# Four attention layers on one core: the second layer's first query chunk cut into four key parts

## The chip, the cores and the metric

One core of a Trainium2 chip runs the whole program. The metric is device time in microseconds (us) of one execution, and the figure of a kernel is the median of several executions.

## The reference

Four residual attention layers follow each other on x of 2048 x 640, with 32 heads of width 20. Layers 0 and 2 use the weights A and a sliding window of 256 keys; layers 1 and 3 use the weights B and attend to all 2048 keys.

```python
x = x + A(layernorm(x)); x = x + B(layernorm(x))
x = x + A(layernorm(x)); x = x + B(layernorm(x))
# A, B: qkv = x @ wqkv; p = softmax(mask(q k^T * 20**-0.5)); out = (p v) @ wo
# mask in A alone: 0 <= i - j < 256
```

## The kernel before

**Work is cut into units.** A unit (layer l, query chunk c, head group g) covers 512 queries (c = 0..3) and four heads (g = 0..7). Its scores are counted in banks: one bank is one head, 128 keys by 512 queries, one PSUM bank of f32. A unit of a windowed layer has 12 banks, a unit of a full layer 64 (16 key blocks of 128, times four heads). The first query chunk of layers 1 and 3 is cut in two parts by `SPLIT`: in layer 1 part "a" has key blocks 0 to 7 and part "b" blocks 8 to 15, 32 banks each.

**The order is one list, `units`, written out by hand.** Before the change: layer 0's chunks 0 to 2; then layer 0's chunk 3, with part "a" of one group of layer 1 after each of its groups 1, 2, 3, 4 and 6; then the three left-over "a" parts; then the eight "b" parts; then layers 1, 2 and 3. A part of layer 1 can start only when its keys exist, and keys of chunk c exist only when layer 0 is finished for that chunk.

**Tiles.** The banks of the list, in order, are cut into tiles of three; while `narrow` holds (layer 0 and part "a"), tiles of three and two alternate. For each tile the scores are made by TensorE (PE, L848), the exp by ScalarE (ACT, L862) straight from PSUM into `pt`, the window mask is multiplied in by VectorE (DVE, L887) in the windowed layers, and two or three tiles later the products with the values are added up in `op`, one single PSUM bank (PE, L905). At the end of a unit `finish_unit` copies `op` away on DVE: part "a" into the f32 tile `raw_o` (L709), part "b" adds it to `raw_o` (L721), other units at L723. The tail then normalises (`t_tail`, L745 to L773).

**Other work hangs between the tiles.** Projections of queries and keys (L323, evacuated by `evac`, L267 on ACT or L269 on DVE), of values (L410), layer norm (L342 to L374) and output projection (L491, L500) are tasks in a list sorted by `need`, the index of the unit that needs them first. After each tile `pump` gives them a credit of `rate(t)`: 1.2 while layer 0 works on chunks 0 to 2, else what it takes to finish the tasks 16 tiles ahead of their need, times 1.1, from 0.66 to 0.9 in the early stage. The credit is in an estimate of full-clock PE microseconds that is written into the tasks. If a unit starts while something that it needs is not made, `require` emits all of that at once, with no tile between. Two PSUM banks, 5 and 6, serve these tasks while tiles are narrow; later only bank 6.

**Layer 1's operands go through DRAM.** `t_full` and `t_v` write queries, keys and values out (L470, L431); `load_unit` brings a part's keys, queries and values back: one DMA for values (L644), four for queries (L655) and four for keys (L657). All these are issued by SyncE's queue (SP), in program order. `load_ahead` looks once per tile at the next unit of a full layer and loads it, if what it needs was made and a buffer is free (three for keys and for values, four for queries).

**Evacuation.** `state["act"]` decides who evacuates projections: ACT while layer 0 is in chunks 0 to 2, DVE from then on.

Of the kernel before, what the change touches and what calls it, by code (L numbers as in the profile page):

```python
# [11 lines left out]
ALU = mybir.AluOpType  # L12
# [7 lines left out]
NT = S // P  # L20
KD = D // P
G = 8
C = 512
NC = S // C
# [1 line left out]
SCALE = DH ** -0.5  # L26
HD = D // 2
VW = DH + 1
SPLIT = {1: 8, 3: 12}


@with_exitstack
def kernel(
# [10 lines left out]
    nc = tc.nc  # L44
# [44 lines left out]
    op = ps[:, 7, :]  # L89
# [16 lines left out]
    def load_wop(w):  # L106
# [7 lines left out]
        out=ident[:], in_=ident[:], compare_op=ALU.not_equal, fill=1.0,  # L114
# [38 lines left out]
    state = {"tick": 0, "held": None, "credit": 0.0, "early": True, "act": True, "unit": 0}  # L153
# [16 lines left out]
    def push(name, gen, need, left):  # L170
        insort(todo, Task(name, gen, need, left))

    def push_tail(name, gen):
        tails.append(Task(name, gen, 0, 0.0))
# [286 lines left out]
    def t_full(l, n, c, b):  # L461

        while ("xnT", l, c) not in ready:
            yield ("wait", 1)
        yield from room("w")
        wt = yield from take_w(l, n, c, b)
        yield from project(wt, xnT[l, c], staged)
        rows = slice(b * P, (b + 1) * P)
        dst = k_d[l][rows, c * C : (c + 1) * C] if n else q_d[l][c, rows, :]
        nc.sync.dma_start(out=dst, in_=staging.pop())  # L470
        live["w"] -= 1
        used(l, c)
        ready.add(("qk"[n], l, c, b))
# [63 lines left out]
    def push_layer(l, c):  # L537

        need = [first_use(l, c, g) for g in range(G)]
        push(("ln", l, c), t_ln(l, c), need[0], 1.6)  # L540
        if l % 2:
            halves = ((0,), (1,)) if l == 1 else ((0, 1),)
            for h in halves:
                push(("v", l, c, *h), t_v(l, c, h), need[4 * h[0]], 2.8 * len(h))
            for b in range(KD):
                g = b * P // 80
                for n in (1, 0):
                    worder[l, n].append((l, n, c, b))
                    first = need[g] if n else index[l, c, g, "a" if c == 0 else None]
                    push(("qk"[n], l, c, b), t_full(l, n, c, b), first, 1.1)  # L550
            return
        for g in range(G):
            for n in (0, 1):
                worder[l, n].append((l, n, c, g))
            push(("qk", l, c, g), t_qk_window(l, c, g), need[g], 2.2)
            if g == 0:
                push(("v", l, c), t_v(l, c, (0, 1)), need[0], 5.6)


    def key_blocks(l, part):  # L560
        return {None: (0, NT), "a": (0, SPLIT.get(l)), "b": (SPLIT.get(l), NT)}[part]

    class Unit:
        def __init__(self, l, c, g, part=None):
# [43 lines left out]
            (1, 2, [(2, 2, 2, 2)]),  # L608
        ]

    units = [Unit(0, c, g) for c in range(NC - 1) for g in range(G)]
    early = deque(Unit(1, 0, g, "a") for g in range(G))
    for g in range(G):
        units.append(Unit(0, NC - 1, g))
        if g in (1, 2, 3, 4, 6):
            units.append(early.popleft())
    units += early
    units += [Unit(1, 0, g, "b") for g in range(G)]
    for c in range(1, NC + 1):
        small = deque(Unit(2, c - 1, g) for g in range(G))  # L620
        for g in range(G):
            units.append(Unit(1, c, g) if c < NC else Unit(3, 0, g, "a"))
            for _ in range(((0, 0, 2, 2, 2, 2, 0, 0) if c < NC else (0, 0, 2, 3, 3, 0, 0, 0))[g]):
                units.append(small.popleft())
    units += [Unit(3, 0, g, "b") for g in range(G)]
    units += [Unit(3, c, g) for c in range(1, NC) for g in range(G)]
    full = [u for u in units if not u.windowed]
    place = {id(u): n for n, u in enumerate(full)}
    index = {(u.l, u.c, u.g, u.part): n for n, u in enumerate(units)}

    def first_use(l, c, g):

        if l % 2 == 0:
            return index[l, c, g, None]
        return index[l, 0, g, "a" if 4 * c < SPLIT[l] else "b"]

    def load_unit(u):

# [62 lines left out]
    part_o = {}  # L701

    def finish_unit(u):
        l, c, g = u.l, u.c, u.g
        if u.part == "a":
            if not part_o:
                part_o["t"] = big.tile([P, G, C], F32, name="raw_o", tag="early_late")
            raw_o = part_o["t"]
            nc.vector.tensor_copy(out=raw_o[:, g, :], in_=op)  # L709
            return  # L710
        if (l, c) not in ons:
            for ll, cc in list(ons):
                if len(ons) >= 2:
                    require(("out", ll, cc))
            ons[l, c] = onp.tile([P, G, C], BF16, name="on", tag="on")
        on = ons[l, c]
        while len(tails) >= 3:
            require(("tail", *tails[0].name[1:]))
        oT = otp.tile([P, C], BF16, name="oT", tag="oT")
        if u.part == "b":  # L720
            nc.vector.tensor_tensor(out=oT[:], in0=part_o["t"][:, g, :], in1=op, op=ALU.add)  # L721
        else:
            nc.vector.tensor_copy(out=oT[:], in_=op)  # L723
        push_tail(("tail", l, c, g), t_tail(l, c, g, on, oT))
# [59 lines left out]
    def t_stats0(c):  # L784
        for i in range(4):
            stats(0, c, i)
            yield ("pe", 0.1)
        ready.add(("x", 0, c))

    with tc.manual_schedule():  # L790
# [3 lines left out]
        require(("qk", 0, 0, 0))  # L794

        def narrow(u):
            return u.l == 0 or (u.l, u.part) == (1, "a")

        banks = [b for u in units for b in u.banks]
        tiles = []  # L800
# [1 line left out]
        n = 0  # L802
# [7 lines left out]
        def rate(t):  # L810

            u = tiles[t][0][0]
            if u.l == 0 and u.c < NC - 1:
                return 1.2
            done, r = 0.0, 0.6 if state["early"] else 0.35
            for task in todo:
                done += max(task.left, 0.0)
                if task.need < len(units):
                    r = max(r, done / max(starts[id(units[task.need])] - t - 16, 1))
            return min(1.1 * r, 0.9)  # L820

        started = set()
        pts = deque()
# [1 line left out]
        for t in range(len(tiles) + 8):  # L825
            state["tick"] += 1
            n_b = 0
            if t < len(tiles):
                cur = tiles[t]
                n_b = len(cur)  # L830
                for b in cur:
                    u = b[0]
                    if id(u) not in started:
                        started.add(id(u))
                        if u.l == 0 and u.g == 0 and u.c + 1 < NC and u.c not in pushed:
                            pushed.add(u.c)
                            push(("stats", u.c + 1), t_stats0(u.c + 1), index[0, u.c + 1, 0, None], 0.4)
                            push_layer(0, u.c + 1)
                        state["unit"] = index[u.l, u.c, u.g, u.part]
                        state["act"] = u.l == 0 and u.c < NC - 1  # L840
                        if state["early"] and not narrow(u):
                            end_early()
                        start_unit(u)
                sp = ps[:, 0:3, :] if t % 2 == 0 else ps[:, 3:6, :]
                for n in range(2):
                    for i, (u, j, m, b0, subs, first, last, end) in enumerate(cur):
                        for kc, q0, qn, col in subs[n : n + 1]:
                            nc.tensor.matmul(  # L848
                                sp[:, i, col * P : (col + qn) * P],
                                lhsT=u.k(kc, j), rhs=u.q(j, q0, qn), start=True, stop=True,  # L850
                            )
                for b in cur:
                    if b[-1]:
                        s_emitted(b[0])
                pt = ptp.tile([P, 3, C], BF16, name="pt", tag="pt")
                i = 0
                while i < n_b:
                    b0 = cur[i][3]
                    k = i
                    while k < n_b and cur[k][3] == b0:  # L860
                        k += 1
                    nc.scalar.activation(  # L862
                        out=pt[:, i:k, b0 * P :], in_=sp[:, i:k, b0 * P :],
                        func=ACT.Exp, scale=SCALE,
                    )
                    i = k
                for i, b in enumerate(cur):
                    pts.append((t, pt, i, b))
                load_ahead()
                r = rate(t)  # L870
                pump(r, r + 0.1)
            else:
                pump(2.0, 2.0)

            if 0 < t <= len(tiles):
                cur_, pt_ = masked
                i = 0
                while i < len(cur_):
# [4 lines left out]
                    if m is not None:  # L883
# [4 lines left out]
                            out=pt_[:, i:k, b0 * P :], in0=pt_[:, i:k, b0 * P :], in1=mv_,  # L888
                            op=ALU.mult,
# [5 lines left out]
            if len(pts) >= 4 and pts[3][0] <= t - (3 if pts[0][3][0].windowed else 2):  # L895
                group = [pts.popleft() for _ in range(4)]
                u, subs, end = group[0][3][0], group[0][3][4], group[3][3][7]
                first, last = group[0][3][5:7]
# [50 lines left out]
```

The softmax here doesn't subtract the row's maximum and nothing guards it: scores larger than these inputs give would overflow.

## Time and profile before

| | |
|---|---|
| median of 4 runs | 2542.0 us (2521.11 to 2548.67) |
| the profiled execution | 2535.62 us |
| its span, first to last instruction | 2533.9 us |
| PE / ACT / DVE busy | 2096.8 / 2259.5 / 831.1 us |
| exp instructions on ACT (L862) | 1695, 2201.2 us |
| moved over the DMA queues | 118.78 MB |

The profile's rows name engines (PE is TensorE, PEld its weight loads, DVE VectorE, ACT ScalarE, POOL GpSimd, SP SyncE) and lines (L862 is line 862 of the kernel). PEclk is the granted TensorE clock, 1.00 or 10 tenths being full speed. A row by stretches gives start and end in us, the length, then the busy time and the number of instructions of each engine, the clock and the DMA share. The matmuls' ends are modelled, so that a busy PE isn't PE at its peak.

Unit ends are seen as DVE's copies of `op`. By these, layer 0's chunk 0 is finished at 102.3 us, its unit (chunk 1, group 4) at 151.0, the second unit of its chunk 3 at 286.9, its last unit at 414.6; the eight "a" parts at 474.8, the first "b" part at 493.7 and all eight at 594.8.

### The profile page before, as it was taken

The numbers are of one execution on the slowest core, as the hardware profiler recorded it, in microseconds if no ns is written. First come the engines' busy times: TensorE is split into PE (matmuls) and PEld (weight loads), VectorE is DVE, ScalarE is ACT, GpSimd is POOL, SyncE is SP. The second block draws the span as 40 slices with busy tenths as digits, with TensorE's granted clock in tenths as the row PEclk, the third lists the DMA queues.
The fourth block names the chain that finished last, engine by engine and source line by source line (L and its number), as shares of the span: only waits on it lengthen the run. The fifth ranks groups of instructions, "written<-read, shape, count | busy, mean of one in ns | idle before, by whom it ended". The sixth has DMA issues, their size and how long they took to land.

```text
span 2533.9 us, 37494 instructions
## 1 busy us (share of the span) xinstructions
PE 2096.8 (83%) x15184; PEld 727.4 (29%) x15184; DVE 831.1 (33%) x1895; ACT 2259.5 (89%) x1819; POOL 39.4 (2%) x112
## 2 busy tenths in 40 slices
PE   7888998888888888788888888888877787777777
PEld 3344333222222333223322233232222222222222
DVE  5676664212333334243334333442210011001001
ACT  5777788799889898999888988898999999999997
POOL 1000000000000000000000000000000000000000
PEclk9899997756755689658885579668565555557556
DMA  4111431311200113002221032103210011001000
GB/s 146 55 33 43 115 82 42 86 39 44 61 23 25 36 43 98 23 25 51 57 69 35 1 86 73 33 11 82 59 32 25 25 37 34 24 25 35 24 25 11
DMA packets 134974, 118.78 MB, mean 47 GB/s; under 512 B 64528, under 2 KB 122256, under 8 KB 134800
## 3 DMA queue, kind: packets, MB, share of 16 engines
q1 hardware_dynamic: 134800, 116.38, 17.1%
q8 instruction: 119, 1.95, 0.3%
q14 instruction: 55, 0.45, 0.1%
HBM read 95.09 MB, written 21.23 MB: 46 GB/s over the span
## 4 chain that ended last, share of the span: by engine, by line
ACT 44%; PE 28%; issue 12%; DVE 6%; DMA 0%; SPq 0%; ACTq 0%; POOL 0%; DVEq 0%
ACT pt L862 43%; PE ps L323 8%; PE ps L848 7%; PE ps L905 5%; PE ps L491 4%; PE ps L410 3%; DVE pt L887 2%; PE ps L374 1%; DVE st L269 1%; PE ps L769 1%; DVE qa L269 0%; DVE oT L723 0%; PE ps L522 0%; DVE ka L269 0%; DVE x_sb L500 0%
## 5 line engine op out<-in xcount | busy, mean ns | idle before, releaser
L862 ACT ACTIVATE pt<-ps 128x1536 bf16<-128x1536 f32 (+2 forms) x1695 | 2201.2, 1531 | 215.7 <-PE ps L848 192.8
L848 PE MATMUL ps<-qt,kt 20*128 20x512 bf16 x4096 | 739.6, 521 | 300.4 <-ACT pt L862 288.4
L905 PE MATMUL ps<-pt,vt 128*21 128x512 bf16 x4096 | 551.2, 524 | 9.2 <-DVE oT L723 5.2
L848 PEld LDWEIGHTS <-kt 20*128 20x128 bf16 x4096 | 206.4, 96 | 784.1 <-issue 769.2
L323 PE MATMUL ps<-xnT,wqk 128*128 128x512 bf16 x1040 | 318.0, 448 | 17.2 <-DMA wqk<-in_B_wqkv_dram 3.4
L887 DVE TENSOR_TENSOR pt<-pt,masks 128x1024 bf16<-128x1024 bf16 (+5 forms) x404 | 240.2, 624 | 218.2 <-ACT pt L862 217.8
L723 DVE CAST oT<-ps 128x512 bf16<-128x512 f32 x112 | 76.8, 685 | 443.8 <-PE ps L905 443.3
L905 PEld LDWEIGHTS <-vt 128*21 128x21 bf16 x4096 | 107.9, 92 | 347.9 <-issue 344.9
L491 PE MATMUL ps<-wop,on 128*128 128x320 bf16 x968 | 179.0, 336 | 3.8 <-DVE x_sb L500 1.9
L848 PE MATMUL ps<-qa,ka 32*128 32x384 bf16 (+2 forms) x1408 | 139.9, 328 | 37.4 <-ACT pt L862 31.9
L323 PEld LDWEIGHTS <-wqk 128*128 128x128 bf16 x1040 | 100.1, 108 | 170.8 <-issue 106.4
L500 DVE TENSOR_TENSOR x_sb<-x_sb,ps 128x320 bf16<-128x320 bf16 x120 | 58.2, 486 | 227.9 <-PE ps L491 227.5
L410 PE MATMUL ps<-wv,xnT 128*128 128x320 bf16 x640 | 120.2, 328 | 9.2 <-ACT xnT L267 2.1
L773 DVE TENSOR_TENSOR on<-oT,ps 128x512 bf16<-128x512 bf16 x128 | 87.7, 685 | 95.7 <-PE ps L769 94.1
L491 PEld LDWEIGHTS <-on 128*128 128x128 bf16 x968 | 94.7, 107 | 74.8 <-issue 32.2
L905 PE MATMUL ps<-pt,va 128*21 128x384 bf16 (+2 forms) x1408 | 92.5, 333 | 14.4 <-DVE oT L723 12.7
L269 DVE CAST st<-ps 128x512 bf16<-128x512 f32 x76 | 52.5, 690 | 127.7 <-PE ps L323 125.6
L750 DVE RECIPROCAL rz<-ps 128x16 f32<-128x16 f32 x128 | 32.8, 256 | 179.1 <-PE ps L745 168.8
L848 PEld LDWEIGHTS <-ka 32*128 32x128 bf16 x1408 | 41.3, 97 | 122.7 <-issue 112.3
L410 PEld LDWEIGHTS <-xnT 128*128 128x128 bf16 x640 | 59.9, 104 | 55.6 <-issue 31.9
L769 PE MATMUL ps<-rT,spread 32*128 32x128 bf16 x512 | 67.5, 270 | 4.4 <-DVE rT L762 3.9
L769 PEld LDWEIGHTS <-spread 32*128 32x128 bf16 x512 | 48.9, 118 | 27.9 <-issue 24.1
(54 smaller groups left out, 649.7 us busy)
## 6 DMA issues: line engine op xcount, KB each, us to landing
wqk<-wqk_d SPq DMA_DIRECT2D x112, 160.0 KB
vt<-v_d SPq DMA_DIRECT2D x48, 336.0 KB
kt<-k_d SPq DMA_DIRECT2D x192, 80.0 KB
wqk<-in_B_wqkv_dram SPq DMA_DIRECT2D x80, 160.0 KB
qt<-q_d SPq DMA_DIRECT2D x320, 20.0 KB
v_d<-vs SPq DMA_DIRECT2D x16, 336.0 KB
k_d<-st SPq DMA_DIRECT2D x40, 128.0 KB
q_d<-st SPq DMA_DIRECT2D x40, 128.0 KB
```

The source lines that it names most:

```text
L269: nc.vector.tensor_copy(out=out_, in_=in_)
L323: nc.tensor.matmul(pq, lhsT=wt[:, dc, :], rhs=xt[:, dc, :], start=(dc == 0), stop=(dc == KD - 1),)
L410: nc.tensor.matmul(pv, lhsT=xt[:, dc, i * P : (i + 1) * P], rhs=wv_sb[l % 2][:, dc, h * HD : (h + 1) * HD], start=(dc == 0), stop=(dc == K ...
L491: nc.tensor.matmul(yp, lhsT=on[:, g, qb * P : (qb + 1) * P], rhs=wop[:, g, i * HD : (i + 1) * HD], start=(last or g == 0), stop=(g == G - 1),)
L500: nc.vector.tensor_tensor(out=xv, in0=had, in1=yp, op=ALU.add)
L723: nc.vector.tensor_copy(out=oT[:], in_=op)
L769: nc.tensor.matmul(zb[:, qb * P : (qb + 1) * P], lhsT=spread4[:, qb, :], rhs=rT[:], start=True, stop=True,)
L773: nc.vector.tensor_tensor(out=on[:, g, :], in0=oT[:], in1=zb, op=ALU.mult)
L848: nc.tensor.matmul(sp[:, i, col * P : (col + qn) * P], lhsT=u.k(kc, j), rhs=u.q(j, q0, qn), start=True, stop=True,)
L862: nc.scalar.activation(out=pt[:, i:k, b0 * P :], in_=sp[:, i:k, b0 * P :], func=ACT.Exp, scale=SCALE,)
L887: nc.vector.tensor_tensor(out=pt_[:, i:k, b0 * P :], in0=pt_[:, i:k, b0 * P :], in1=mv_, op=ALU.mult,)
L905: nc.tensor.matmul(op[32 * j : 32 * j + VW, q0 * P : (q0 + qn) * P], lhsT=u.v(kc, j), rhs=pt[:, i, col * P : (col + qn) * P], start=(first ...
```

## The change

The two-way split of layer 1's first chunk becomes four parts of four key blocks, each as long as one query chunk of layer 0. Parts 0, 1 and 2 of all eight groups (24 units of 16 banks) are put one by one behind layer 0's units, from chunk 1, group 5 on; 19 find a place there and the other five follow, then the eight parts 3. Layer 3's split stays as it was. A part takes its keys from one chunk alone, so that part 0 can start when layer 0's chunk 0 is through.

With it come: `raw_o` is added to by the middle parts; tiles stay narrow for parts 0 to 2; the flat credit of 1.2 and the evacuation on ACT end at the first woven part (before: at layer 0's chunk 3); and the credit's upper end is 1.0 instead of 0.9 while a layer-0 unit is on.

```diff
-SPLIT = {1: 8, 3: 12}
+PARTS = {
+    l: [(e[n], e[n + 1]) for n in range(len(e) - 1)]
+    for l, e in ((1, (0, 4, 8, 12, 16)), (3, (0, 12, 16)))
+}
...
-    units = [Unit(0, c, g) for c in range(NC - 1) for g in range(G)]
-    early = deque(Unit(1, 0, g, "a") for g in range(G))
-    for g in range(G):
-        units.append(Unit(0, NC - 1, g))
-        if g in (1, 2, 3, 4, 6):
-            units.append(early.popleft())
+    units = [Unit(0, 0, g) for g in range(G)]
+    early = deque(Unit(1, 0, g, p) for p in PARTS[1][:3] for g in range(G))
+    for c in range(1, NC):
+        for g in range(G):
+            units.append(Unit(0, c, g))
+            if (c, g) >= (1, 5):
+                units.append(early.popleft())
     units += early
-    units += [Unit(1, 0, g, "b") for g in range(G)]
+    units += [Unit(1, 0, g, PARTS[1][3]) for g in range(G)]
...
-            raw_o = part_o["t"]
-            nc.vector.tensor_copy(out=raw_o[:, g, :], in_=op)
+            raw_o = part_o["t"][:, g, :]
+            if u.part[0] == 0:
+                nc.vector.tensor_copy(out=raw_o, in_=op)
+            else:
+                nc.vector.tensor_tensor(out=raw_o, in0=raw_o, in1=op, op=ALU.add)
...
-            return u.l == 0 or (u.l, u.part) == (1, "a")
+            return u.l == 0 or (u.l == 1 and u.part in PARTS[1][:3])
+
+        woven = index[1, 0, 0, PARTS[1][0]]
...
-            if u.l == 0 and u.c < NC - 1:
+            if index[u.l, u.c, u.g, u.part] < woven:
                 return 1.2
...
-            return min(1.1 * r, 0.9)
+            return min(1.1 * r, 1.0 if u.l == 0 else 0.9)
...
-                        state["act"] = u.l == 0 and u.c < NC - 1
+                        state["act"] = state["unit"] < woven
```

More of the change, by code (lines that the diff above doesn't have):

```diff
@@ L548, in push_layer @@
                     worder[l, n].append((l, n, c, b))
-                    first = need[g] if n else index[l, c, g, "a" if c == 0 else None]
+                    first = need[g] if n else index[l, c, g, PARTS[l][0] if c == 0 else None]
                     push(("qk"[n], l, c, b), t_full(l, n, c, b), first, 1.1)
@@ L560, in key_blocks @@
     def key_blocks(l, part):
-        return {None: (0, NT), "a": (0, SPLIT.get(l)), "b": (SPLIT.get(l), NT)}[part]
+        return part or (0, NT)
     class Unit:
@@ L621 @@
         for g in range(G):
-            units.append(Unit(1, c, g) if c < NC else Unit(3, 0, g, "a"))
+            units.append(Unit(1, c, g) if c < NC else Unit(3, 0, g, PARTS[3][0]))
             for _ in range(((0, 0, 2, 2, 2, 2, 0, 0) if c < NC else (0, 0, 2, 3, 3, 0, 0, 0))[g]):
                 units.append(small.popleft())
-    units += [Unit(3, 0, g, "b") for g in range(G)]
+    units += [Unit(3, 0, g, PARTS[3][1]) for g in range(G)]
     units += [Unit(3, c, g) for c in range(1, NC) for g in range(G)]
@@ L634, in first_use @@
             return index[l, c, g, None]
-        return index[l, 0, g, "a" if 4 * c < SPLIT[l] else "b"]
+        return next(index[l, 0, g, p] for p in PARTS[l] if 4 * c < p[1])
     def load_unit(u):
@@ L704, in finish_unit @@
         l, c, g = u.l, u.c, u.g
-        if u.part == "a":
+        if u.part and u.part[1] < NT:
             if not part_o:
                 part_o["t"] = big.tile([P, G, C], F32, name="raw_o", tag="early_late")
-            raw_o = part_o["t"]
-            nc.vector.tensor_copy(out=raw_o[:, g, :], in_=op)
+            raw_o = part_o["t"][:, g, :]
[3 more added lines that the diff above has]
+                nc.vector.tensor_tensor(out=raw_o, in0=raw_o, in1=op, op=ALU.add)
             return
@@ L719, in finish_unit @@
         oT = otp.tile([P, C], BF16, name="oT", tag="oT")
-        if u.part == "b":
+        if u.part:
             nc.vector.tensor_tensor(out=oT[:], in0=part_o["t"][:, g, :], in1=op, op=ALU.add)
```

## The prediction

> **What bounds the kernel now.** I read the page's slices first, then busy time by stage, then the timeline inside one stage, then the groups by shape.
>
> ```profile
> PE 2096.8 (83%) x15184; PEld 727.4 (29%) x15184; DVE 831.1 (33%) x1895; ACT 2259.5 (89%) x1819; POOL 39.4 (2%) x112
> ...
> PE   7888998888888888788888888888877787777777
> ...
> ACT  5777788799889898999888988898999999999997
> ...
> PEclk9899997756755689658885579668565555557556
> ```
>
> ACT, with its exps, carries most of the span, but not at the start: in the first seven slices (63 us each) ACT is 5 to 8 tenths busy while PE is 7 to 9 tenths busy at a clock of 8 to 9 tenths. The stages, cut at the unit ends given above:
>
> ```profile
> core 0: us, PE busy (x) PEld busy (x) DVE busy (x) ACT busy (x) POOL busy (x), PEclk, DMA share, GB/s
> ...
> 102.30:151.00 48.70, 44.62 (x441) 21.06 (x440) 35.02 (x82) 37.85 (x45) 0.39 (x3) 0.92 0.12 35
> 151.00:286.90 135.90, 118.32 (x1136) 53.61 (x1134) 97.25 (x228) 100.70 (x117) 6.60 (x14) 0.94 0.19 52
> 286.90:394.10 107.20, 99.64 (x827) 39.51 (x824) 67.58 (x139) 88.90 (x75) 1.83 (x4) 0.98 0.38 102
> 394.10:414.60 20.50, 16.36 (x124) 4.21 (x122) 6.87 (x16) 19.58 (x18) 0.00 (x0) 0.50 0.09 22
> 414.60:474.80 60.20, 52.17 (x350) 20.72 (x348) 22.42 (x51) 44.43 (x38) 1.82 (x4) 0.81 0.29 70
> 474.80:493.70 18.90, 16.17 (x88) 4.31 (x85) 3.38 (x6) 15.93 (x12) 0.00 (x0) 0.68 0.24 67
> 493.70:594.80 101.10, 81.53 (x517) 23.42 (x515) 16.06 (x45) 99.66 (x75) 0.00 (x0) 0.52 0.14 39
> 594.80:2533.90 1939.10, 1591.06 (x11137) 526.30 (x11136) 518.70 (x1174) 1785.26 (x1338) 14.58 (x40) 0.66 0.15 40
> ```
>
> Two stages with opposite limits stand side by side. From 151 to 394 PE is the limit, at nearly full clock (87% and 93% busy). From 493.7 to 594.8, the "b" parts, ACT is busy 99.66 of 101.1 us and PE could do far more: its clock is half (0.52). The change moves banks from the second kind of stage into the first. Nothing after 594.8 is reordered.
>
> **What moves.** Before layer 0's last unit ends, the old list has five "a" parts of 32 banks, 160; the new one has 18 parts of 16 banks, 288. Between that and the last stage both have 96 banks (three "a"; six of part 2). The last stage falls from 256 banks to 128. So exactly 128 banks leave the ACT-bound stage and enter the PE-bound one.
>
> **Taken away.** The stage 493.7 to 594.8 has 75 tiles of three, 101.1 / 75 = 1.348 us each. 128 banks are 42.7 such tiles: 42.7 x 1.348 = **57.5 us off the path**.
>
> **Put in.** In narrow tiles (2.5 banks on average) they make 51.2 tiles. What one costs PE at full clock is seen in the timeline:
>
> ```profile
> 427.02 0.39 PE L848 MATMUL ps<-qt,kt 20*128 20x512 bf16 x3
> 427.34 0.40 PE L905 MATMUL ps<-pt,vt 128*21 128x512 bf16 x4
> ...
> 427.67 0.39 PE L848 MATMUL ps<-qt,kt 20*128 20x512 bf16 x2
> 427.99 1.26 PE L491 MATMUL ps<-wop,on 128*128 128x320 bf16 x8
> ```
>
> Read start to start: scores 0.32, products of four banks 0.33. A tile: 0.32 + 0.33 x 2.5/4 = 0.53 us; 51.2 x 0.53 = 27 us of PE. From 151.0 to 414.6 PE is busy 118.3 + 99.6 + 16.4 = 234.3 of 263.6 us, 89%. The new sum is 261.5. At the share of now (0.89) the stretch takes 294 us, at that of the stage that already weaves (286.9 to 394.1, 0.93) 281; the bounds of the cost are 0 (ACT's 54 idle us there swallow it all, no PE wait is lengthened) and 58 (each tile adds a whole ACT period, 20.5 / 18 = 1.14 us, as from 394 to 414). I take 0.91, between the two measured shares: 287.4, **+23.8 us**. The task work in the stretch is the same in both kernels, only laid out anew: per tile it gets thinner, over some 206 tiles instead of 155.
>
> ACT doesn't take over as the limit: 100.7 + 88.9 + 19.6 = 209.2 us busy, minus the copies that leave it, plus 51.2 x 1.12 = 57 (half of tiles at 1.33, half about 0.9, scaled from it) gives under 240 of 287. The copies: ACT's evacuations (L267) between 151 and 286.9 are 55 and fill 30.1 us; they go to DVE at up to 0.69 each, 36 us. DVE then has 97.3 + 67.6 + 6.9 = 171.8, plus 36, plus the adds below: 216 of 287, 75%. It was at 72% from 151 to 286.9; hidden at the price of somewhat later task banks, inside the 0.91.
>
> **Unit ends.** The eight copies of part "a" become 24 copies and adds, 16 more. The nearest rows:
>
> ```profile
> L709 DVE COPY raw_o<-ps 128x512 f32<-128x512 f32 x16 | 10.9, 684 | 1.1 <-PE ps L905 1.1
> L721 DVE TENSOR_TENSOR oT<-raw_o,ps 128x512 bf16<-128x512 f32 x16 | 10.9, 684 | 48.4 <-PE ps L905 48.4
> ```
>
> An add with the f32 tile costs what the copy costs, 684 ns; 16 x 0.684 = 11 us of DVE. On PE the first products of the next unit wait, since `op` is one bank: PE's waits for L709 are 1.6 us over 16 of them, 0.1 each, and at most 0.69. 16 x 0.1 to 16 x 0.69 is 1.6 to 11; taken 2.6, near the measured row, since PE is fuller here.
>
> **Loads.** 32 parts instead of 16 are loaded: 16 x 9 = 144 more DMAs (64 each for queries and keys, 16 for values), 0.33 us of SP each, 48 us of SP over some 350. They are hidden where `load_ahead` runs a unit ahead, one every 28 banks. SP works in order: a key load that waits for its write to land keeps weight loads (`wqk`) behind it waiting, and PE's next projections with them. How much lead is there? From the end of layer 0's chunk to the first part that needs it: part 0 72 banks, parts 1 and 2 168 each, part 3 96. Before: 120 for "a", 96 for "b". Only part 0 is tighter; its 72 banks lie in windowed units that take 48.7 us for five units now, so about 57 us, against 60.2 us that the last chunk has now. One late arrival is on the chain of waits already, at the old first "a" part:
>
> ```profile
> 276.51 0.02 SPq L657
> ...
> 276.56 2.25 DMA kt<-k_d
> ...
> 278.85 0.23 PE ps L848 x2
> ```
>
> It costs 2.25 us, with the evacuation ahead of it (0.70) 3. I charge the new first part **3 us** (0: it takes the place of the old one; 15 if its five key blocks each come late).
>
> **The clock.** The Trainium skill (TensorE: Matmul & The Clock Gate, HAM oscillation) says that PE falls to half clock after an idle gap of about 3.4 us. By that rule the woven stretch, whose gaps are far shorter, keeps full clock all through, and the sum stands. The trace differs: from 394.1 to 414.6 PE is 80% busy with no such gap, and the clock is 0.50. So the clock also sinks where ACT is the limit and tasks are out. With the row in place of the rule, a third of the 51.2 tiles (where tasks run out) cost 1.14 instead of 0.53 us: +10 us. I keep the 0.91 and put the 10 into the range.
>
> **Sum.** -57.5 + 23.8 + 2.6 + 3 = -28.1. The profiled execution took 2535.6 (span 2533.9 and 1.7 around it): 2507.5. The median of the runs shown is 6.4 higher, 2542.0: **2514 us**, 1.1% less. About 1% is what a measurement of this kernel can tell from no change.
>
> **Rivals.** (1) *Uneven tasks.* The credit can run at its upper end of 1.0 and then run out. By the exps counted between unit ends, 23 tiles took 35.7 us (1.55 each) from 358 to 394, with much task work, and 1.14 each right after, with nearly none. By such swings instead of an even 1.36 I estimate 0.12 us more a tile, 206 x 0.12 = 25: nearly all is given back, 2539. For it: the window 394 to 414. Against: 287 to 358 held 1.35 (53 in 71.5 us) under the same pacing. (2) *Each key chunk's chain comes onto the path (slower).* Output projection, norm, keys and values of a chunk, write and read back, now set the pace at 414.6 to 474.8: 60.2 us with ACT busy 44.4, so 15.8 us are lost. If parts 0, 1 and 2 each paid that, 47.4 more: 2514 + 47 = 2561; with part 0's five key blocks late by 3 us each, 2576. It decides from two such boundaries on (28 / 15.8). Against: the lead of 168 banks. (3) *PE fills up entirely*, ACT's idle time takes the woven tiles for nothing: 2542 - 52 = 2490.
>
> **How the numbers follow.** As summed, 2497 to 2527: 0.60, of which 0.40 lie below 2516.6, 1% under the median. Rival 3: 0.06, faster. Rival 1: 0.18, within 1%. Rival 2: 0.16, of which 0.12 over 2567.4. Faster 0.46, same 0.42, slower 0.12. The range leaves out rival 2's upper part and the far end of rival 3: 2490 to 2554.
>
> **What would show it.** Right: eight last parts in about 62 us instead of 120; layer 0's end at about 440 us instead of 415, PE over 0.9 busy there at a clock over 0.9; the eight last parts through near 567 us instead of 594.8; behind it 1939 us as before. Wrong: waits of L848 for `kt` above some us, ACT idle more than 10 us ahead of a part's first tile, many projections in a row with no tile between, or the later stage longer, because tasks (queries of chunks 1 to 3) were left for it.

## The result, and the profile after

The changed kernel takes 2527.7 us (median of 43 runs, 2520.51 to 2540.02) against 2539.29 for the kernel before in the same sessions: a ratio of **0.9959, 95% interval 0.9948 to 0.9969**. It is faster by 0.41%, some 10.4 us by the ratio. The forecast was 28 us, 1.1%. The direction is right, the size is not.

The profiled executions, one of each, differ by less than the medians: spans of 2531.8 after and 2533.9 before. Single executions spread over some 20 us (after) and 29 us (before), so the profile shows where time goes better than how much is gained in all.

First the slices of the page, as before: one digit for each 63 us.

```profile
PE 2104.0 (83%) x15184; PEld 730.1 (29%) x15184; DVE 873.2 (34%) x1969; ACT 2231.9 (88%) x1769; POOL 38.0 (2%) x112
...
PE   6878999888888898878888889788877787777777
...
ACT  5746888879889888898988988999999999999997
...
PEclk9888999776765679656886589758565565557556
```

From the fifth to the eighth slice ACT is at 8 where it was at 7 or 8. But the third slice (127 to 190 us) has fallen from 7 to 4. Busy times by stretches, again cut at unit ends: layer 0's chunk 0; chunk 1 to group 4; its group 5 alone; the woven stretch to layer 0's end in two rows; the left-over parts 2; parts 3; the rest.

```profile
core 0: us, PE busy (x) PEld busy (x) DVE busy (x) ACT busy (x) POOL busy (x), PEclk, DMA share, GB/s
...
103.40:150.20 46.80, 42.80 (x429) 19.97 (x428) 37.17 (x90) 35.82 (x40) 2.37 (x7) 0.91 0.07 19
150.20:188.10 37.90, 25.80 (x143) 11.94 (x141) 14.82 (x34) 5.38 (x5) 0.00 (x0) 0.68 0.21 49
188.10:295.90 107.80, 93.45 (x783) 36.84 (x780) 73.68 (x161) 80.14 (x68) 3.64 (x10) 0.86 0.19 53
295.90:473.50 177.60, 163.00 (x1426) 61.87 (x1424) 120.50 (x248) 155.18 (x134) 1.82 (x4) 0.88 0.29 76
473.50:533.20 59.70, 52.44 (x351) 20.98 (x350) 24.41 (x54) 44.36 (x39) 1.82 (x4) 0.81 0.33 78
533.20:596.30 63.10, 55.44 (x348) 16.56 (x345) 19.04 (x48) 58.14 (x44) 0.00 (x0) 0.55 0.24 67
596.30:2531.80 1935.50, 1594.10 (x11138) 527.69 (x11135) 518.72 (x1175) 1785.70 (x1338) 14.55 (x40) 0.66 0.15 40
```

The last parts take 63.1 us instead of 120.0: the saving came. The six parts before them (the 19th of the woven ones and the five that follow) take 59.7 us, as the 60.2 of before. The rest is 1935.5 against 1939.1. The excess is between 150.2 and 473.5: 323.3 us, where 263.6 stood before and 293 were forecast (287.4 and the terms of 2.6 and 3). And 37.9 us of that are one single unit, layer 0's chunk 1, group 5, which took 8.0 us before (151.0 to 159.0). In it ACT is busy for 5.4 us. ACT's own timeline there:

```profile
150.15 1.45 ACT L872 ACTIVATE pt<-ps 128x1536 bf16<-128x1536 f32 x1 [0.30 <-PE ps L858]
151.50 0.58 ACT L271 CAST qa<-ps 128x512 bf16<-128x512 f32 x1
181.55 1.02 ACT L872 ACTIVATE pt<-ps 128x1024 bf16<-128x1024 f32 x1 [29.47 <-PE ps L858]
```

ACT waits 29.47 us in one piece, and the scores it waits for (L858) are those of the first woven part. The chain of waits tells what stood ahead of them:

```profile
153.59 2.96 PE ps L414 x20
...
158.50 0.47 PE ps L378 x5
...
162.26 4.73 PE ps L414 x20
167.02 0.51 DVE vs L273
...
168.04 3.17 DMA wqk<-in_B_wqkv_dram
...
171.26 4.46 PE ps L327 x10
175.74 0.70 DVE st L273
176.46 1.72 DMA q_d<-st
...
180.79 1.63 DMA kt<-k_d
```

The row at 153.59 still belongs to layer 0: values of its chunk 2. What follows is the chain of layer 1's chunk 0, emitted at once: layer-norm transposes (L378), values (L414 at 162.26), the weights that are fetched only now (3.17 us), keys and queries (L327), written out (1.72), read back (1.63). PE is busy for 25.8 of the 37.9 us. Its clock is 0.68 on average there, and 0.50 while the ten projections run (171.2 to 175.8 us), so that each takes about 0.45 us. This is `require`: the part starts and what it needs was not made. In program order 94 task matmuls stand between the scores of two tiles there: 50 of chunk 0's chain, 35 of layer 0's own projections, 9 of a tail. The kernel before has, behind its first tiles, no more than 30 in one place.

### The profile page after: what moved, and what is told of

The parts are those of the page before. It is cut to its first block, busy times and chain, and to the rows that moved or that the text cites. A ratio compares the mean times of both kernels' runs of the same rounds, so it can differ in the third digit from the quotient of the medians.

```text
span 2531.8 us, 37668 instructions
## 1 busy us (share of the span) xinstructions
PE 2104.0 (83%) x15184; PEld 730.1 (29%) x15184; DVE 873.2 (34%) x1969; ACT 2231.9 (88%) x1769; POOL 38.0 (2%) x112
## 4 chain that ended last, share of the span: by engine, by line
ACT 42%; PE 37%; issue 12%; DVE 8%; DMA 1%; SPq 0%; POOL 0%; ACTq 0%; DVEq 0%; POOLq 0%
ACT pt L872 42%; PE ps L327 11%; PE ps L858 9%; PE ps L915 6%; PE ps L495 5%; PE ps L414 4%; DVE pt L897 2%; PE ps L378 1%; PE ps L777 1%; DVE st L273 1%; DVE oT L731 1%; DVE qa L273 0%; DVE xn L369 0%; DVE ka L273 0%; DVE stats L347 0%
## 5 line engine op out<-in xcount | busy, mean ns | idle before, releaser
L858 PE MATMUL ps<-qt,kt 20*128 20x512 bf16 x4096 | 736.4, 514 | 289.6 <-ACT pt L872 273.3
L915 PE MATMUL ps<-pt,vt 128*21 128x512 bf16 x4096 | 545.7, 518 | 8.9 <-DVE oT L731 6.2
L858 PEld LDWEIGHTS <-kt 20*128 20x128 bf16 x4096 | 204.8, 96 | 764.2 <-issue 740.6
L327 PE MATMUL ps<-xnT,wqk 128*128 128x512 bf16 x1040 | 324.4, 455 | 21.4 <-DMA wqk<-in_B_wqkv_dram 11.7
L495 PE MATMUL ps<-wop,on 128*128 128x320 bf16 x968 | 189.4, 350 | 3.7 <-DVE on L781 2.3
L858 PE MATMUL ps<-qa,ka 32*128 32x384 bf16 (+2 forms) x1408 | 144.8, 338 | 35.8 <-ACT pt L872 33.7
L327 PEld LDWEIGHTS <-wqk 128*128 128x128 bf16 x1040 | 100.4, 109 | 183.2 <-issue 111.5
L414 PE MATMUL ps<-wv,xnT 128*128 128x320 bf16 x640 | 122.5, 333 | 4.0 <-DVE vs L273 1.0
L858 PEld LDWEIGHTS <-ka 32*128 32x128 bf16 x1408 | 42.2, 98 | 124.5 <-issue 119.7
L414 PEld LDWEIGHTS <-xnT 128*128 128x128 bf16 x640 | 60.4, 105 | 52.4 <-issue 27.9
L378 PE MATMUL ps<-ident,xn 128*128 128x128 bf16 x320 | 39.8, 280 | 24.6 <-DVE xn L369 22.2
```

The lines of the kernel that those rows point to most:

```text
L327: nc.tensor.matmul(pq, lhsT=wt[:, dc, :], rhs=xt[:, dc, :], start=(dc == 0), stop=(dc == KD - 1),)
L378: nc.tensor.transpose(out=trp[:, dc, :], in_=xn[:, dc * P : (dc + 1) * P], identity=ident[:])
L414: nc.tensor.matmul(pv, lhsT=xt[:, dc, i * P : (i + 1) * P], rhs=wv_sb[l % 2][:, dc, h * HD : (h + 1) * HD], start=(dc == 0), stop=(dc == K ...
L495: nc.tensor.matmul(yp, lhsT=on[:, g, qb * P : (qb + 1) * P], rhs=wop[:, g, i * HD : (i + 1) * HD], start=(last or g == 0), stop=(g == G - 1),)
L858: nc.tensor.matmul(sp[:, i, col * P : (col + qn) * P], lhsT=u.k(kc, j), rhs=u.q(j, q0, qn), start=True, stop=True,)
L915: nc.tensor.matmul(op[32 * j : 32 * j + VW, q0 * P : (q0 + qn) * P], lhsT=u.v(kc, j), rhs=pt[:, i, col * P : (col + qn) * P], start=(first ...
```

## The experiments

The theory after the result, A: this one burst is the missing time. The rival, B: the stretch is PE-bound, the burst's matmuls have to be paid anyway, and the put-in banks cost as much as the last stage saves. The kernels ran in three sessions (e0 to e3; e4, e5, e7 and e8; e9 to e12), each beside the kernel before, whose medians there were 2538.8, 2538.9 and 2537.1 us. A ratio is always to the kernel before of the same session; there are 4 to 22 executions of each kernel.

### Is it the burst? Three ways round it

**e0_again**: the changed kernel unaltered.

> The changed kernel once more, as control and for a second profile. Theory A (one burst of 94 matmuls for chunk 0's norm, values, keys and queries, emitted at once ahead of the first woven part, costs the missing time): the time is again about 0.996 of before, the unit ahead of the first woven part again takes some 38 us, with ACT idle 25 to 30 us in one piece. Theory B (the PE-bound stretch pays for woven banks what the last stage saves, with or without the burst): the same time; the 38 us could then be shorter with nothing gained at the end.

Measured: 2525.3 us, ratio 0.996 (0.9942 to 0.9978). The unit again takes 36.0 us (155.0 to 191.0), with an idle piece of ACT of 27.8 us. The burst is a property of the program, not of one execution.

**e1_from_17**:

```diff
-            if (c, g) >= (1, 5):
+            if (c, g) >= (1, 7):
```

> Weaving starts two units later (after chunk 1, group 7), so that chunk 0's chain has 96 banks of lead instead of 72; two fewer parts find a place in layer 0. Theory A: the burst falls from 94 to 25 matmuls, ACT's idle piece from 29 us to under 8, worth 17 to 20 us; two parts more at the end cost some 7 us: 10 to 13 us faster than the changed kernel, 0.991 to 0.992 of before. Theory B: nothing comes of the shorter burst, the two parts cost 4 to 7 us: 0.997 to 0.999 of before.

Measured: 2506.2 us, ratio 0.9888 (0.985 to 0.9926), 19 us faster than e0_again, more than the 10 to 13 that A gave. ACT's longest idle piece is 8.5 us.

**e2_ln2**, the limit on chunks that are in the layer norm at a time:

```diff
-    cap = {"qa": 3, "ka": 18, "va": 10, "xnT": 5, "kt": 3, "vt": 3, "qt": 4, "ln": 1, "w": 4, "vs": 2}
+    cap = {"qa": 3, "ka": 18, "va": 10, "xnT": 5, "kt": 3, "vt": 3, "qt": 4, "ln": 2, "w": 4, "vs": 2}
```

> All as in the change, but two chunks may be in the layer norm at a time instead of one, so that layer 1's chunk 0 need not wait for layer 0's chunk 2. Theory A: burst 34 instead of 94 matmuls, ACT's idle piece under 12 us, 10 to 17 us faster than the changed kernel, 0.989 to 0.992 of before. Theory B: within 3 us of the changed kernel.

Measured: 2506.9 us, ratio 0.9892 (0.985 to 0.9934); longest idle piece 14.4 us, a little over the forecast 12. The order of units is that of e0_again, so that the two profiles can be laid side by side, chunk 1 from the end of its group 4; first e0_again, then e2:

```profile
155.00:226.90 71.90, 53.29 (x379) 21.92 (x384) 35.93 (x76) 31.19 (x27) 0.00 (x0) 0.86 0.29 74
```

```profile
154.70:209.30 54.60, 44.83 (x353) 17.81 (x353) 30.19 (x62) 32.88 (x29) 0.00 (x0) 0.91 0.32 80
```

Here 17.3 us are gained. Layer 0's chunks 2 and 3, the last parts 2 and the parts 3 differ by at most 2.2 us each, the rest by 3.5 the other way. So the gain stands where the burst stood.

**e3_credit**:

```diff
-                return 1.2
+                return 1.6 if u.c else 1.2
```

> All as in the change, but the tasks' credit per tile is 1.6 instead of 1.2 while layer 0 is in chunk 1 and no part is woven yet: chunk 0's chain is emitted between tiles. Theory A: no burst, the stretch up to the first woven part 10 to 17 us shorter, 0.989 to 0.992 of before. Theory B: the tiles ahead of it get longer by what the burst gets shorter, within 4 us of the changed kernel.

Measured: 2511.0 us, ratio 0.9906 (0.9871 to 0.9942); longest idle piece 7.7 us, while the tiles ahead of it got longer: chunk 1, group 4 is through at 162.9 instead of 155.0 us.

Three different edits, which all shorten the burst, gain 19.1, 18.4 and 14.2 us over e0_again. B, which gave at most 4, falls. The forecast had 28 us and the change brought 10.4: the missing 18 us are about what comes back.

**e12_before_ln2**, the control for e2: the same edit in the kernel before.

> The kernel before with two chunks in the layer norm and nothing else: control for e2 and e8. If e2's gain over the change comes of the shorter burst ahead of the first woven part, this has nothing to gain: ratio 0.998 to 1.002. If two norms at a time are faster by themselves: 0.993 or less, as e2 stands to the change.

Measured: 2538.2 us, ratio 0.9996 (0.9975 to 1.0016). In the kernel before, two norms at a time gain nothing.

### Less of the burst still, and more parts inside layer 0

**e8_from17_ln2**: the edits of e1 and e2 together.

> Start as in e1 and two chunks in the layer norm as in e2: no burst of 24 or more matmuls is left ahead of the first part. If the length of the burst is what costs: 2 to 6 us faster than e1, 2500 to 2504 us, ACT's idle piece ahead of the first part under 5 us. Rival, the earlier norm takes PE and DVE time from layer 0's own projections: no faster than e1 (2506).

Measured: **2496.8 us, ratio 0.9841 (0.9794 to 0.9888)**, the fastest kernel here by the medians, 9 us ahead of e1 and 31 ahead of the change. It has four executions only, and its interval overlaps that of e1. The longest idle piece is 4.3 us. It gained more than the 2 to 6 us of the forecast, and more than the 4.2 us by which that piece shrank. Layer 0's chunk 3, with the very same units, takes 111.5 us in e8 and 126.4 in e1; first e1, then e8:

```profile
318.60:445.00 126.40, 109.69 (x948) 42.63 (x954) 81.48 (x171) 104.04 (x89) 2.47 (x4) 0.87 0.24 61
```

```profile
318.90:430.40 111.50, 102.45 (x961) 41.14 (x969) 83.57 (x174) 102.99 (x89) 1.82 (x4) 0.97 0.32 83
```

ACT and DVE are as long busy; PE's clock is 0.97 instead of 0.87. Up to 422 us ACT waits 17.7 us for scores in e1 and 5.9 in e8. One hole in e1 is at 350 to 358 us, with PE busy 4.6 of 8 us at a clock of 0.71, and there a layer norm is on the chain of waits. From 422 to 445 us e1 has ACT as the limit, busy 22.7 of 23.0 us, with the clock at 0.50. So its work is crowded at the front of the stretch and thin at its end, and in e8 it is more even. That the earlier norm does this is what the two traces suggest; no run separates it.

**e11_from16_ln2**: start after chunk 1, group 6, with e2's edit.

> Start after chunk 1, group 6, two chunks in the layer norm: between e2 and e8, with one more part inside layer 0 than e8. A burst of 49 matmuls stands ahead of the first part here, 34 in e2 and none of 24 in e8. If the burst is what costs: slower than e8 by 4 to 12 us, 2501 to 2509. If the number of parts inside layer 0 is what counts: 2 to 4 us faster than e8, 2493 to 2495.

Measured: 2504.3 us, ratio 0.986 (0.9832 to 0.9887). One part more inside layer 0 than e8 and a burst of 49: 7.5 us slower by the medians and 4.8 by the ratios, on the side of the burst, but the two intervals overlap.

**e4_from17_double**:

```diff
+            if (c, g) in ((3, 2), (3, 3)):
+                units.append(early.popleft())
```

on top of e1.

> Weaving starts after chunk 1, group 7 as in e1, but two parts instead of one follow layer 0's chunk 3, groups 2 and 3, so that 19 parts again find a place in layer 0. By the prices of the prediction 32 banks leave the ACT-bound end (10.7 tiles at 1.348 = 14.4 us) and enter the PE-bound stretch (12.8 tiles at 0.465 = 6.0 us): 8 us faster than e1, about 2498 us. Rival, a full PE: each tile put in costs its whole 1.14 us, 14.6 us, and the time stays that of e1, 2506.

Measured: 2522.0 us, ratio 0.9937 (0.992 to 0.9955): 16 us *slower* than e1, where the prices of the prediction gave 8 faster and the rival the same. Layer 0's chunk 3 (for e1 the first row under e8), the left-over parts 2, parts 3; first e1, from the parts 2 on, then e4:

```profile
445.00:516.20 71.20, 64.25 (x432) 24.07 (x433) 28.38 (x60) 59.44 (x51) 1.82 (x4) 0.84 0.36 84
516.20:575.40 59.20, 50.53 (x328) 15.21 (x325) 16.29 (x45) 57.85 (x44) 0.00 (x0) 0.50 0.21 57
```

```profile
320.80:465.40 144.60, 120.85 (x1007) 44.78 (x1016) 83.55 (x173) 118.46 (x102) 2.47 (x4) 0.83 0.22 57
465.40:524.60 59.20, 51.69 (x349) 20.79 (x350) 24.40 (x54) 44.34 (x39) 1.82 (x4) 0.82 0.33 79
524.60:589.50 64.90, 56.86 (x346) 16.66 (x345) 19.08 (x49) 58.28 (x44) 0.00 (x0) 0.53 0.25 65
```

Putting 13 more tiles into chunk 3 cost 18.2 us, 1.4 a tile (102 exps instead of 89). Taking them out of the end gave 12.0 us, and the last parts took 5.7 back. Against e1 that makes 11.9 us slower. The traces show two causes of the 18.2 us. At the end of chunk 3 ACT is the limit already in e1 (422 to 445 us, above), and in e4 it is busy 35.0 of 35.4 us from 430.0 to 465.4, with 32 exps, 1.1 us each: more tiles there find nothing idle. And at 396.7 us ACT is idle for 5.3 us, where PE waits 4.1 us for weights (`wqk`), which it does not in e1. In the parts 3 ACT waits 11.0 us for scores, in e1 4.3; that the tiles which left had covered the last chunk's chain is a guess that no run tests.

### The other parts of the change

**e7_cut_alone**: the kernel before, only cut finer. Both halves of an old part stand together (`early` holds parts 0 and 1 of a group; the lines left out put credit, evacuation and narrow tiles back to what they were):

```diff
...
+    early = deque([Unit(1, 0, g, p) for p in PARTS[1][:2]] for g in range(G))
+    for g in range(G):
+        units.append(Unit(0, NC - 1, g))
+        if g in (1, 2, 3, 4, 6):
+            units += early.popleft()
+    for two in early:
+        units += two
+    units += [Unit(1, 0, g, p) for g in range(G) for p in PARTS[1][2:]]
...
```

> The kernel before with layer 1's first chunk cut into four parts, and nothing moved: parts 0 and 1 stand in the place of the old first part, parts 2 and 3 in that of the second; credit and evacuation as before. It measures what the 16 more unit ends and 144 more DMAs cost by themselves. Prediction: 2.6 us (0.16 a unit end, loads hidden), ratio to before 1.001. Rival: each unit end costs the whole 0.69 us copy and each third load comes late by 2.25: 11 plus 12 us, ratio 1.009.

Measured: 2534.0 us, ratio 0.998 (0.996 to 1.0). No cost can be seen: the interval ends at 1.0, so the forecast 2.6 us (1.001) was if anything too much, and the rival's 23 us are excluded.

**e5_ln2_oldevac**, on top of e2:

```diff
-        woven = index[1, 0, 0, PARTS[1][0]]
+        woven = index[0, NC - 1, 0, None]
```

> e2 with two parts of the change undone: ACT evacuates, and the flat credit of 1.2 stays, up to layer 0's chunk 3 as in the kernel before. Theory of the prediction: where the copies go is hidden (ACT and DVE are 81 and 75% busy), the flat credit makes tasks come early and then run out, which the prediction priced at 0.12 us a tile: over some 120 tiles up to 14 us slower than e2, 2510 to 2521. Rival: since the tasks come earlier, the chains of chunks 1 and 2 have more lead, and it is as fast as e2 (2507) or faster.

Measured: 2542.7 us, ratio 1.0011 (0.9994 to 1.0028): 36 us slower than e2, outside both forecasts. The whole gain is gone. Two runs take the two parts by themselves.

**e10_ln2_flatcredit**, on top of e2:

```diff
-            if index[u.l, u.c, u.g, u.part] < woven:
+            if index[u.l, u.c, u.g, u.part] < index[0, NC - 1, 0, None]:
                 return 1.2
```

> e2 with only the flat credit of 1.2 up to layer 0's chunk 3; DVE evacuates from the first woven part on. If the credit is what costs in e5: 2530 to 2543, tasks done early and PE's clock at 0.5 to 0.7 where they have run out (320 to 366 us). The prediction's price of uneven tasks, 0.12 us a tile over some 120 tiles, gives 14 us: 2521. If the copies cost: within 6 us of e2.

Measured: 2537.8 us, ratio 0.9996 (0.9979 to 1.0012), 31 us slower than e2. Here are three stretches of e10 through its chunk 2:

```profile
180.00:240.00 60.00, 55.67 (x436) 23.22 (x436) 41.93 (x90) 39.93 (x35) 1.21 (x2) 0.89 0.28 75
240.00:300.00 60.00, 54.22 (x445) 23.57 (x444) 43.49 (x94) 38.44 (x32) 2.38 (x8) 0.89 0.29 74
300.00:366.00 66.00, 54.97 (x429) 18.86 (x428) 35.31 (x70) 51.80 (x45) 0.00 (x0) 0.74 0.19 52
```

Up to 300 us PE is the fuller engine (93 and 90% busy) and ACT is busy about two thirds: in the second row 60 / 32 = 1.9 us for each of its instructions. Then the tasks are out, ACT goes up to 78% and PE's clock falls to 0.74. e2, with paced credit, takes 124.7 us from the end of chunk 1 to that of chunk 2 (209.3 to 334.0), e10 150.4 (215.5 to 365.9).

**e9_ln2_oldcopies**, on top of e2:

```diff
-                        state["act"] = state["unit"] < woven
+                        state["act"] = state["unit"] < index[0, NC - 1, 0, None]
```

> e2 with only the copies as before: ACT evacuates up to layer 0's chunk 3; the credit stays paced. e5, with both parts undone, was 36 us slower than e2. If the copies are what costs there: most of the 36 us, 2530 to 2543, with ACT the fuller engine in the woven stretch. If the credit costs: within 6 us of e2, 2501 to 2513, as the prediction has it (copies hidden on either engine).

Measured: 2518.3 us, ratio 0.9909 (0.9878 to 0.9941), 11 us slower than e2 by the medians. That lies between the two forecasts, and the interval overlaps that of e2, so this part is not settled; by the medians it is a third of e5's loss. The third small part of the change, the credit's upper end of 1.0 instead of 0.9, was not taken by itself.

## Why the prediction was right in direction and wrong in size

- **The step that failed: "I charge the new first part 3 us (0: it takes the place of the old one; 15 if its five key blocks each come late)".** Where the first woven part stands, a unit took 37.9 us that took 8.0 before. Not all of these 30 us are lost, since the burst's matmuls have to be made somewhere; with the burst shortened by three edits, 14 to 19 us come back. The first figure is twice the term's own upper bound of 15, the second is at it or above, since I thought of late loads (2.25 us each) and not of a chain that isn't begun. The prediction even lists the sign (ACT idle over 10 us ahead of a part's first tile, many projections in a row with no tile between), but gave it no cost in the sum. The lead was judged by its length alone: 57 us, nearly the 60.2 that the last chunk has (the trace left 48, from 103.4 to about 151.5). But in the last stretch no work of layer 0 is left that could compete with the chain; in chunk 1 layer 0's own projections come ahead of it by `need`, and the norm of layer 0's chunk 2 held the only place in the norm (`"ln": 1`): its transposes (L378) are seen on PE at 105.8, 108.6, 139.1 and 142.9 us. Output projection of chunk 0 ended at 134 us, layer 1's norm reached PE at 157 us, after the part should have started. That one place is in the code, and the prediction didn't look at it.
- **Taken away, 57.5 us:** the last stage fell from 120.0 to 63.1 us, 56.9. Right.
- **Put in, 23.8 us:** with the burst shortened, the sum holds as a mean: e2's stretch from chunk 1, group 4 to layer 0's end is 297.5 us (154.7 to 452.2), of which 14.4 are still one idle piece; forecast were 287.4, plus 2.6 and 3. But it is no price per tile. In e8 96 more banks than before (38.4 tiles) cost 10.0 us (273.6 against 263.6), 0.26 a tile; in e4 13 tiles in the last chunk of the same stretch cost 1.4 each, outside my upper bound of 1.14, part of it the wait for weights. (A reading of the prediction is off by a slice: the clock of 8 to 9 tenths holds for the first six slices, the seventh has 7.)
- **Unit ends, 2.6 us, and loads at nothing:** in e7 loads and unit ends together cost nothing that can be seen (0.998). The add with `raw_o` takes what the copy takes:

```profile
L717 DVE TENSOR_TENSOR raw_o<-raw_o,ps 128x512 f32<-128x512 f32 x16 | 10.9, 681 | 1.0 <-PE ps L915 0.9
```

- **Copies on DVE, hidden:** e9 leans the other way, to a gain of some 11 us from moving them, without being clear of noise.
- **Rival 1, uneven tasks, 25 us:** not needed for the missing time, but the mechanism is real and larger than priced: on e2 the flat credit costs 31 us (e10), where this price gave 14. The pacing that comes with the change is a condition of the gain, and the prediction passed over it as "laid out anew".
- **Rival 2, each chunk's chain on the path:** right for part 0 and only there. Behind its burst part 0 has two more idle pieces of ACT, 6.1 and 4.2 us; parts 1 and 2, with 168 banks of lead, have none over 3.5. It was priced at 15.8 us a boundary; the three edits won back 14 to 19 at this one.
- **The clock:** the rule of the Trainium skill (TensorE: Matmul & The Clock Gate, HAM oscillation) speaks of idle gaps of some 3.4 us. By it the clock of the burst would fall only in its two long waits (4.28 us for weights, 4.51 for keys). It did fall in the first of them, near 169.6 us, and stayed at 0.50 to 186 us. But it had fallen before: it is 0.50 from 160 to 166 us, where from 150 us on no wait of PE was over 0.94 us; from 156 to 160 us PE was 56% busy. In e8 it also fell, to 0.58 and 0.50 from 422 to 438 us, with PE busy 83% of the time. The measurement decides: such a gap is not needed.

## What to carry to other kernels

When work is moved ahead to fill an idle engine, follow back what its first piece needs, through every queue and every "one at a time" on the way, and count what stands in front of it there; a lead in microseconds says little when other work has the same lead. In this kernel two more units of lead together with a second place in the norm turned a gain of 0.4% into one of 1.6%. Here filling worked only while there was idleness of the right kind to fill and background work was dealt out evenly: the same parts with a flat credit gained nothing, and two parts more in the last chunk of the stretch made it slower.

## What the runs showed of the hardware that was not expected

PE's clock does not wait for long gaps to fall: it is 0.50 at 80% busy where ACT sets the pace (before, 394.1 to 414.6 us, where no wait of PE is over 0.6 us), and 1.00 at 93% busy in the woven stretch of e8 (318.9 to 422 us). The two shares can't be compared as they stand, since busy time grows as the clock falls: three score matmuls take 0.54 us start to start in the first stretch (395.33 to 395.87) and 0.32 at full clock. By this ratio, as an estimate, the 80% would be 47% at full clock. At which share the clock turns the runs don't show. The burst of the change therefore cost twice: PE waits in it, and its matmuls then run at the lower clock (ten projections take 4.46 us there; five take 1.19 to 1.25 at full clock, so ten would take 2.4 to 2.5).
